# Range tests of the weights on their high halves and later in the order; the first chunk's scores of both halves in pairs

## The chip, the core and the metric

One core of a Trainium2 chip. The metric is the device time of one execution in microseconds; three runs of the kernel before gave 1187.11, 1194.1 and 1196.09, median 1194.1.

## The reference, cut to what matters

Three parts follow each other. First a recurrence over 768 steps for 4 x 8 heads, each with a 40 x 40 state:

```
for t in range(S):
    y[t]  = einsum('d,de->e', r[t], state)
    Sa    = einsum('de,e->d', state, a[t])
    state = state * w[t][None, :] - outer(Sa, b[t]) + outer(v[t], k[t])
```

Its output, laid out as 3072 tokens x 320, goes through two dense layers without normalisation. The first is `h = x @ w_in; g = h * cos(h); x = g @ w_out` with 2048 hidden values, the second `h = x @ w_in2; g = s * max(h, 0)**2 + b; out = g @ w_out2`.

## The kernel before, in words

The recurrence is computed in 12 chunks of 64 steps. A chunk is prepared (decay products by a scan on DVE, scaled inputs, scores between steps as matmuls, an inverse of a triangular system on DVE), and then goes through a chain that carries the state to the next chunk. The 32 heads stand as two halves of the partitions (rows 0 to 39 and 64 to 103) times two pair groups `pg` times eight; a "g" is one half of one pair group. `prep` lists the preparation, `chain` the chain. Behind the chain the 64 x 4 tokens of the chunk are stored (`xs`), reloaded (`x1_load`) and go through the first dense layer (`m1_f`: the product with `w_in`, cosine, split in high and low halves; `m1_s`: the product with `w_out`). The second dense layer (`x2`, `m2_f`, `m2_s`) runs when all chunks are through.

Matmuls run in float16 with operands split in a high and a low half, except for chunk 0, whose scores, transposes and chain use float32 operands of 40 rows directly. For chunk 0, `sc1` (k, b against a) and `sc2` (the transposed result XT against r) are run once for each g, eight matmuls of 40 x 128 weights and 64 columns, all on one half of the rows.

The weights arrive as 64-bit floats. `float32` rebuilds 32-bit words on DVE with three integer instructions, in place; `w_in_chunk` and `w_out_chunk` then take a range test, copy the high half (ACT), scale (POOL) and subtract to get the low half (POOL or DVE). The range test is a Square on ACT with a running sum into `st`; for `w1` the squares also feed short matmuls with a vector of ones (`norm`, PSUM tile `np`) and a maximum on DVE. The sums are looked at once, at the end (`verdict`), to choose between this program and a slow one. Raw chunks lie partly in the place of the final weights and partly in four buffers of the tag "xs", which also holds the reloaded tokens.

The order of the work is written out by a planner, `Recorder`, when the program is built: every operation gets an estimated duration, a priority (its longest path to the end) and the time at which its inputs are there; `schedule` picks, engine by engine, the operation that can start first, by priority where several can. The engines then run their lists strictly in that order, and SP issues all transfers in one order. `caps` limits how many tiles of a class live at once ("XT": 2), out of shared buffers such as the eight of tag "q". All recorded instructions carry line 392 of the program, so rows are told apart by tile names: `w`, `v`, `wraw`, `vraw` are weights, `junk` the sink of squares, `s1p` and `s2p` the scores of `sc1` and `sc2`, `txp` and `XT` the transposes before `sc2`, `hp` and `op` the two products of a dense layer, `q`, `gh`, `gl` the hidden values and their halves, `yhl` the halves of y, `x` the stored tokens.

Of the kernel before, what the change touches and what calls it, by code (L numbers as in the profile page):

```python
# [24 lines left out]
C = 64  # L25
# [63 lines left out]


class _Op:
    __slots__ = ("eng", "calls", "dur", "lat", "blk", "preds", "succ", "npred", "prio", "ready", "tiles", "start", "end", "idx", "mm", "cols")


class Recorder:
# [5 lines left out]
    def __init__(self, nc, caps):  # L101
        self.real, self.caps = nc, caps
        for e in self.ENG:
            setattr(self, e, _Engine(self, e))
        self.ops, self.blk = [], -1
        self.base = {}
        self.sink = set()
        self.blk_tiles = {}
        self.key = {}
        self.acc = {}  # L110
        self.use = {}
        self.free = {}
        self.n_bufs = {}
        self.live_cls = {}
        self.order = {}
        self.t_eng = dict.fromkeys(self.ENG, 0.0)
        self.done_blk = set()
        self.todo = []
        self.cols = {}
        self.t_dma = 0.0  # L120

    def pool(self, p, name):
        return _Pool(self, p, name)
# [26 lines left out]
    @staticmethod  # L150
    def cost(eng, method, out, ins, k):
        size = lambda x: math.prod(c for _, c in list(x.ap)[1:])
        n = size(out)
        psum = any(x.space == PSUM for x in ins)
        if eng == "tensor":

            k, m, f = ins[0].ap[0][1], size(ins[0]), 1 + (ins[0].dtype == F32)
            if method == "transpose":
                return k * f, m * f, k / 128, k * f * f
            low = Recorder.region(out)[0] < 64  # L160
            n, side = size(ins[1]) * f * f, 2 if m <= 64 else 1
            return n if low else 0, (32 if m == 128 and f == 1 else m * f * f) / side, k / 128, n / side
        if eng == "scalar":
            return (0.05 if psum else 0.092) + n * 0.833e-3 + (0.093 if k.get("accum_out") is not None else 0) + \
                (0.093 if isinstance(k.get("bias"), bass.AP) else 0)
        if eng == "vector":
            if method == "reciprocal":
                return 0.065 + n * 6.3e-3
            if method == "tensor_tensor_scan":
                return 0.065 + n * 2.08e-3  # L170
            if method == "transpose":
                return 0.065 + n * 1.87e-3
            if method == "tensor_reduce":
                return 0.065 + size(ins[0]) * 1.04e-3
            half = method in ("tensor_scalar", "tensor_copy", "memset") and not (psum and ins[0].dtype == F32)
            return 0.065 + n * (0.52e-3 if half else 1.04e-3) + (0.063 if isinstance(k.get("scalar"), bass.AP) else 0)
        if eng == "gpsimd":
            if method in ("tensor_scalar", "memset"):
                return 0.05 + n * (1.03e-3 if method == "tensor_scalar" else 0.8e-3)
            return 0.147 + n * (2.1e-3 if out.dtype == F32 else 1.887e-3)  # L180
        b = WIDTH.get(out.dtype, 4) * math.prod(c for _, c in out.ap)
        run = min(Recorder.run(x) for x in (out, *ins) if x.ap[-1][0] == 1)
        full = max(x.ap[0][1] for x in (out, *ins) if x.space != DRAM) == 128
        return 0.45 if full else 0.625, b / (360e3 if run >= 512 else 180e3)
# [11 lines left out]
    def add(self, eng, method, f, a, k):  # L196
# [7 lines left out]
        if not (op is not None and eng == "tensor" and op.eng == eng and op.blk == self.blk):  # L204
            op = _Op()
            op.eng, op.calls, op.dur, op.lat, op.blk = eng, [], 0.0, 0.0, self.blk
            op.preds, op.succ, op.tiles, op.ready, op.idx = {}, [], set(), 0.0, len(self.ops)
            op.start = op.end = None
            self.ops.append(op)
            self.todo.append(op)  # L210
            op.mm, op.cols = [], 0
        op.calls.append((f, a, k))
        if eng == "sync":
            op.dur, op.mm = c
# [60 lines left out]
    def schedule(self, until=None):  # L275
# [22 lines left out]
        while n_left and left:  # L298
            best = None
            for e in self.ENG:  # L300
                te = self.t_eng[e]
                pick = None
                for o in ready[e]:
                    est = max(o.ready, te)
                    if o.blk not in self.done_blk:
                        s = self.slots(o.blk)
                        if s is None:
# [124 lines left out]
class Fast:  # L432
# [5 lines left out]
    def consts(self, p):  # L438
# [14 lines left out]
        self.st = p.tile([128, len(STATS), 2 * NC], F32, name="st")  # L453
        nc.gpsimd.memset(self.st, 0.0)
        self.tmin = p.tile([128, 2, 16], F32, name="tmin")
        self.junk = p.tile([128, 512], BF16, name="junk")
        self.neg1 = p.tile([128, 1], F32, name="neg1")
        nc.gpsimd.memset(self.neg1, -1.0)
        self.half_pi = p.tile([128, 1], F32, name="half_pi")
# [100 lines left out]
    def w_in_chunk(self, dst, name, k, n, lo):  # L560
        nc = self.nc
        raw = self.RAW["i", k]
        st = self.float32(raw)
        if name == "w1":
            sq = raw.bitcast(BF16)[..., 0::4]
            nc.scalar.activation(sq, st, AF.Square, accum_out=self.st[0:120, STAT_IX[name], k:k + 1])
            self.norm(self.ones, [sq[0:j, i] for i, j in enumerate((120, 120, 80))], k, 1)
        else:
            for q in (0, 2):
                self.square(st[:, q:min(q + 2, 3)], name, 2 * k + q // 2)  # L570
        m = n // 128
        wv = dst[:, k * m:k * m + m].rearrange("p f a n -> p a f n")
        sv = st.rearrange("p a (f n) -> p a f n", f=m)
# [6 lines left out]
    def w_out_chunk(self, dst, name, k):  # L580
        nc = self.nc
        st = self.float32(self.RAW["o", k])
        self.square(st, name, k)
        nc.scalar.activation(dst[:, k, 0], st, AF.Copy, scale=SW)
        if name == "v2" and k % 4 < 2:
            nc.vector.scalar_tensor_tensor(out=dst[:, k, 1], in0=st, scalar=SW, in1=dst[:, k, 0], op0=ALU.mult, op1=ALU.subtract)
            return
        nc.gpsimd.tensor_scalar(out=st, in0=st, scalar1=SW, scalar2=1.0, op0=ALU.mult, op1=ALU.mult)
        nc.gpsimd.tensor_tensor(out=dst[:, k, 1], in0=st, in1=dst[:, k, 0], op=ALU.subtract)

    def weights(self, wn, vn, wd, vd):
        for k in range(0, NFF, 2):
# [21 lines left out]
    def scan(self, c):  # L614
        nc = self.nc
        for q in range(2):
            nc.scalar.activation(self.junk.rearrange("p (l j) -> p l j", j=32), self.X[c][0][:, q * 16:q * 16 + 16, 1:33], AF.Relu,
                                 bias=self.neg1, accum_out=self.st[:, STAT_IX["w"], 2 * c + q:2 * c + q + 1])
        for y, op in zip(self.X[c], (ALU.subtract, ALU.add)):
            y = y.rearrange("p l j -> p (l j)")  # L620
# [112 lines left out]
    def sc1(self, c, g):  # L733
        nc = self.nc
        ps = self.pp.tile([128, 8, C], F32, tag="at", bufs=8, name="s1p")
        for l in range(8):
            if c == 0:
                r = slice(g % 2 * 64, g % 2 * 64 + 40)
                k = self.IN["kb", c, g // 2][r, l].rearrange("p m t -> p (m t)")
                a = self.A0[g // 2, 0][r, l]  # L740
            else:
                k, a = self.KB[c, g][0:120, l, :], self.AR[c, g][0:120, l, 0:C]
            nc.tensor.matmul(ps[:, l, :], k, a, start=(l == 0), stop=True, skip_group_check=True)
        if g == 0:
            self.ND[c] = self.pst.tile([128, 16, 32], F32, tag="ND", name="ND", bufs=1)
        m = self.M1[c, g] = self.pa.tile([128, 8, C], F32, tag="M1", name="M1", bufs=7)
# [177 lines left out]
    def sc2(self, c, g):  # L924
        nc = self.nc
        ps = self.pp.tile([128, 8, C], F32, tag="at", bufs=8, name="s2p")
        for l in range(8):
            if c == 0:
                r = slice(g % 2 * 64, g % 2 * 64 + 40)
                x, ar = self.XT[0, g, l // 4][r, l % 4, :], self.A0[g // 2, 1][r, l, :]  # L930
            else:
                x, ar = self.XT[c, g][0:120, l, :], self.AR[c, g][0:120, l, C:2 * C]
            nc.tensor.matmul(ps[:, l, :], x, ar, start=(l == 0), stop=True, skip_group_check=True)
        m = self.M2[c, g] = self.pm.tile([128, 8, C], F32, tag="q", name="M2", bufs=8)
        nc.vector.tensor_tensor(out=m, in0=ps, in1=bc(self.mask2, 1, [128, 8, C]), op=ALU.mult)

# [180 lines left out]
    def prep(self, c):  # L1117
# [4 lines left out]
        for pg in range(2):  # L1122
# [3 lines left out]
            do(self.stage_ar, c, pg)  # L1126
            do(self.kb_out, c, 2 * pg)
            do(self.kb_out, c, 2 * pg + 1)
            for g in (2 * pg, 2 * pg + 1):
                do(self.tz, c, g)  # L1130
                do(self.sc1, c, g)
        do(self.inv_begin, c)
        do(self.inv, c)
        do(self.inv_out, c)
# [4 lines left out]

    def chain(self, c, pg):  # L1140
        g0, g1 = 2 * pg, 2 * pg + 1
        for f in [(self.rhs, c, pg), (self.u_half, c, pg, 0), (self.lmul, c, pg), (self.u_half, c, pg, 1), (self.uhl, c, g0), (self.uhl, c, g1),
                  (self.sp, c, pg), (self.tx, c, g0), (self.sc2, c, g0), (self.tx, c, g1), (self.sc2, c, g1),
                  (self.yt, c, pg), (self.ts, c, pg)]:
            self.do(*f)

# [11 lines left out]
    def run(self, es0):  # L1158
# [3 lines left out]
        with ExitStack() as es:  # L1162
# [2 lines left out]
            self.x0 = dr.tile([NC, 2, 3, 40, 768], F16, name="x0")  # L1165
            self.x1 = dr.tile([NC, 2, 128, DM], F32, name="x1")
            self.consts(pc)
            rec = self.nc = Recorder(nc, {"any": {"at", "xs", "q"}, "cls": {"XT": 2, "rhp": 3, "hp": 2, "op": 2, "xs": 2, "M2": 2, "q": 4, "att": 6}})
            rec.sink.add(self.junk.tensor.name)
            pool = lambda s, n, **k: rec.pool(s.enter_context(tc.tile_pool(name=n, bufs=1, **k)), n)  # L1170
            self.pm = pool(es, "mlp")
# [13 lines left out]
            for c in range(NC):  # L1185
# [6 lines left out]
                self.do(self.xs, c)  # L1192
                self.do(self.x1_load, c)
                self.mlp(self.m1_f, self.m1_s, c)
            rec.schedule(until=("prep",))
            es_p.close()
            es_v = ExitStack()
# [15 lines left out]
            for j in range(NC):  # L1213
                self.do(self.x2, j)
                self.mlp(self.m2_f, self.m2_s, j)
            rec.schedule()
            es_b.close()
            es_v.close()
# [158 lines left out]
```

## Time and profile before

| | us |
|---|---|
| runs | 1187.11, 1194.1, 1196.09 (median 1194.1) |
| profiled execution, its own time | 1188.45 |
| its span, first to last instruction | 1186.7 |
| busy: PE, weight loads, DVE, ACT, POOL | 1024.5, 822.7, 718.7, 740.1, 437.2 |
| chain that ended last: PE, DVE, DMA, ACT, SP's queue | 57%, 13%, 12%, 7%, 6% |

Busy times are sums over the whole span and don't say where an engine limits the work; the chain of waits gives shares by what was worked on last. Both are averages over stages, which the rows below take apart. A row's idle time is that of its engine just before it, with what ended it.

### The profile page before, as it was taken

How to read it: one execution, taken by the hardware profiler on the slowest of the kernel's cores; microseconds unless marked ns; L12 is line 12 of the kernel's file. 1: busy time of each engine (PE TensorE's matmuls, PEld its weight loads, DVE VectorE, ACT ScalarE, POOL GpSimd, SP SyncE). 2: the span in 40 equal slices, each digit the busy share in tenths (PEclk: the TensorE clock that was granted, in tenths of full speed). 3: DMA queues.
4: the chain of work that ended last, by engine and by line, in shares of the span. 5: the costliest groups of instructions: out<-in, count | busy, mean ns of one | idle time of the engine just before them, and what ended most of it. 6: DMA issues, size and time to landing. Idle time of an engine off the chain costs nothing.

```text
span 1186.7 us, 37912 instructions
## 1 busy us (share of the span) xinstructions
PE 1024.5 (86%) x16094; PEld 822.7 (69%) x16094; DVE 718.7 (61%) x1390; ACT 740.1 (62%) x1640; POOL 437.2 (37%) x430
## 2 busy tenths in 40 slices
PE   3335878988999889989989998976999999999996
PEld 3234767776778677767777776755788888888885
DVE  6989475857573849384846553789444455454543
ACT  4466568786767677677868674766544454444443
POOL 2685455465535464536454512358300000000000
PEclk9999969999999899989998899888999999999999
DMA  9553343444433543253443222475000000000001
GB/s 229 190 193 121 114 151 116 150 126 156 138 101 122 159 144 125 95 172 109 146 137 124 86 68 73 147 185 131 27 23 23 23 23 23 23 23 23 23 13 24
DMA packets 74755, 121.15 MB, mean 102 GB/s; under 512 B 16500, under 2 KB 47348, under 8 KB 73556
## 3 DMA queue, kind: packets, MB, share of 16 engines
q1 hardware_dynamic: 74580, 118.67, 33.1%
q8 instruction: 128, 2.10, 0.8%
q14 instruction: 47, 0.39, 0.1%
HBM read 72.71 MB, written 12.29 MB: 72 GB/s over the span
## 4 chain that ended last, share of the span: by engine, by line
PE 57%; DVE 13%; DMA 12%; ACT 7%; SPq 6%; issue 4%; POOL 0%; ACTq 0%; DVEq 0%; POOLq 0%
PE hp L392 23%; PE op L392 21%; SPq L392 6%; DMA XX<-in_w 4%; PE ytp L392 3%; PE rhp L392 3%; DVE XX L392 3%; DMA wraw<-in_w 3%; DVE wraw L392 2%; DMA XT<-XT 2%; PE uhp L392 2%; DVE v L392 1%; DMA xs<-x 1%; ACT XT L392 1%; DVE w L392 1%
## 5 line engine op out<-in xcount | busy, mean ns | idle before, releaser
L392 PEld LDWEIGHTS <-w 120*128 120x128 f16 (+1 forms) x3102 | 301.1, 100 | 98.8 <-ACT w L392 33.1
L392 PE MATMUL op<-v,gh 128*128 128x320 f16 x1536 | 328.5, 304 | 3.2 <-ACT gh L392 3.0
L392 PE MATMUL op<-v,gl 128*128 128x320 f16 x768 | 232.9, 303 | 2.6 <-POOL gl L392 2.6
L392 PE MATMUL hp<-xs,w 120*128 120x256 f16 x1536 | 208.8, 287 | 11.9 <-DMA xs<-x 10.7
L392 PE MATMUL hp<-x2s,w 120*128 120x256 f16 x1536 | 189.8, 272 | 0.0
L392 POOL TENSOR_TENSOR gl<-q,gh 128x512 f16<-128x512 f32 x96 | 116.9, 1220 | 197.0 <-ACT gh L392 191.8
L392 PEld LDWEIGHTS <-gh 128*128 128x128 f16 x1536 | 144.2, 99 | 52.2 <-ACT gh L392 3.6
L392 ACT ACTIVATE q<-hp 128x512 f32<-128x512 f32 x96 | 57.2, 596 | 126.3 <-PE hp L392 126.0
L392 DVE SCALAR_TENSOR_TENSOR q<-q,s_t 128x512 f32<-128x512 f32 x96 | 72.1, 751 | 102.6 <-ACT q L392 96.8
L392 DVE SCALAR_TENSOR_TENSOR q<-hp,q 128x512 f32<-128x512 f32 x96 | 65.3, 684 | 81.0 <-ACT q L392 78.3
L392 DVE SCALAR_TENSOR_TENSOR gl<-q,b_t,gh 128x512 f16<-128x512 f32 x96 | 72.1, 752 | 48.9 <-ACT gh L392 46.8
L392 PEld LDWEIGHTS <-gl 128*128 128x128 f16 x768 | 75.8, 99 | 35.2 <-POOL gl L392 3.8
L392 ACT ACTIVATE gh<-q,b_t 128x512 f16<-128x512 f32 x96 | 69.1, 720 | 42.9 <-DVE q L392 41.8
L392 DVE TENSOR_TENSOR_SCAN XX<-XX,starts 128x264 f32<-128x264 f32 x96 | 73.1, 816 | 29.2 <-DMA XX<-in_w 28.2
L392 ACT ACTIVATE q<-hp,half_pi 128x512 f32<-128x512 f32 x96 | 65.1, 681 | 36.4 <-PE hp L392 33.7
L392 POOL TENSOR_TENSOR kb<-kb,XX 128x512 f32<-128x512 f32 x44 | 57.6, 1318 | 73.2 <-DVE XX L392 64.1
L392 ACT ACTIVATE gh<-q 128x512 f16<-128x512 f32 x96 | 59.2, 625 | 22.2 <-DVE q L392 20.2
L392 POOL TENSOR_TENSOR kbl<-kb,kbh 128x1024 f16<-128x1024 f32 x22 | 47.5, 2158 | 28.0 <-ACT kbh L392 27.5
L392 ACT ACTIVATE R<-rhp 32x320 f32<-32x320 f32 x96 | 41.1, 428 | 23.1 <-PE rhp L392 21.0
L392 PE MATMUL rhp<-UF,M 64*64 64x40 f32 (+1 forms) x1536 | 53.3, 229 | 0.8 <-ACT UF L392 0.5
L392 DVE TENSOR_TENSOR M<-s2p,mask 128x512 f32<-128x512 f32 x48 | 32.2, 685 | 34.6 <-PE s2p L392 34.5
L392 POOL TENSOR_TENSOR arl<-ar,arh 128x1024 f16<-128x1024 f32 x22 | 48.0, 2180 | 12.3 <-ACT arh L392 12.2
(184 smaller groups left out, 1787.4 us busy)
## 6 DMA issues: line engine op xcount, KB each, us to landing
XX<-in_w SPq DMA_DIRECT2D x12, 1056.0 KB
kb<-in_kb SPq DMA_DIRECT2D x24, 512.0 KB
ar<-in_ar SPq DMA_DIRECT2D x22, 512.0 KB
KB<-kbh SPq DMA_DIRECT2D x88, 80.0 KB
ars<-arh SPq DMA_DIRECT2D x88, 80.0 KB
v<-in_v SPq DMA_DIRECT2D x20, 320.0 KB
wraw<-in_w SPq DMA_DIRECT2D x8, 720.0 KB
SS<-SHL SPq DMA_DIRECT2D x88, 50.0 KB
```

The source lines that it names most:

```text
L392: f(*a, **k)
```

## The change

The range tests leave the conversion of a chunk. New functions read the finished high halves, scaled back, two chunks at a time, and are recorded behind the first dense layer's work for chunk 3 (and, for the second layer, behind chunk 3 of its work), with a field `nb` that tells the planner not to start them before 250 us (750 us) plus 12 us a step, in its own time. For chunk 0, `sc1_0` and `sc2_0` put the matmuls of the two halves of a pair group in turn, into two PSUM tiles; what followed a score group stands in `sc1_end` and `sc2_end`. In the chain of chunk 0 both transposes come ahead of the scores. The class limit of XT is 3, the planner counts two row halves for matmuls of up to 64 rows, and the sink of squares has 640 columns.

```diff
-            n, side = size(ins[1]) * f * f, 2 if m <= 64 else 1
+            n, side = size(ins[1]) * f * f, 2 if m <= 64 or k <= 64 else 1
...
-                    est = max(o.ready, te)
+                    est = max(o.ready, te, o.nb)
...
     def w_in_chunk(self, dst, name, k, n, lo):
         st = self.float32(raw)
-        if name == "w1":
-            sq = raw.bitcast(BF16)[..., 0::4]
-            nc.scalar.activation(sq, st, AF.Square, accum_out=self.st[0:120, STAT_IX[name], k:k + 1])
-            self.norm(self.ones, [sq[0:j, i] for i, j in enumerate((120, 120, 80))], k, 1)
-        else:
-            for q in (0, 2):
-                self.square(st[:, q:min(q + 2, 3)], name, 2 * k + q // 2)
...
     def w_out_chunk(self, dst, name, k):
-        self.square(st, name, k)
...
+    def w_in_test(self, src, name, k):
+        sq = self.pm.tile([120, 2, 3, 128], BF16, tag="xs", name="wsq", bufs=4)
+        for i, (rows, a, n) in enumerate(((120, 0, 2), (80, 4, 1))):
+            nc.scalar.activation(sq[0:rows, :, 2 * i:2 * i + n], src[0:rows, 2 * k:2 * k + 2, a:a + n], AF.Square, scale=1.0 / SW,
+                                 accum_out=self.st[0:rows, STAT_IX[name], 2 * k + i:2 * k + i + 1])
+        if name == "w1":
+            for f in range(2):
+                self.norm(self.ones, [sq[0:j, f, i] for i, j in enumerate((120, 120, 80))], 2 * k + f, 1)
+    def w_out_test(self, src, name, k):
+        self.square(src[:, 2 * k:2 * k + 2, 0], name, k, 1.0 / SW)
+    def tests(self, wn, vn, wd, vd, t):
+        for k in range(NFF // 2):
+            self.nc.nb = t + 12 * k
+            self.do(self.w_in_test, wd, wn, k)
+            self.do(self.w_out_test, vd, vn, k)
+        self.nc.nb = 0.0
...
+    def sc2_0(self, pg):
+        ps = [self.pp.tile([128, 8, C], F32, tag="at", bufs=8, name="s2p") for _ in range(2)]
+        for l in range(8):
+            for hf in range(2):
+                r = slice(hf * 64, hf * 64 + 40)
+                self.nc.tensor.matmul(ps[hf][:, l, :], self.XT[0, 2 * pg + hf, l // 4][r, l % 4, :], self.A0[pg, 1][r, l, :],
+                                      start=(l == 0), stop=True, skip_group_check=True)
+        for hf in range(2):
+            self.sc2_end(0, 2 * pg + hf, ps[hf])
...
+        sc2 = [(self.tx, c, g0), (self.tx, c, g1), (self.sc2_0, pg)] if c == 0 else [(self.tx, c, g0), (self.sc2, c, g0), (self.tx, c, g1), (self.sc2, c, g1)]
...
-            rec = self.nc = Recorder(nc, {..., "cls": {"XT": 2, ...}})
+            rec = self.nc = Recorder(nc, {..., "cls": {"XT": 3, ...}})
...
                 self.mlp(self.m1_f, self.m1_s, c)
+                if c == 3:
+                    self.tests("w1", "v1", self.w1, self.v1, 250)
...
                 self.mlp(self.m2_f, self.m2_s, j)
+                if j == 3:
+                    self.tests("w2", "v2", self.w2, self.v2, 750)
```

`sc1_0` has the form of `sc2_0`, with the scaled k, b as weights and the scaled a as moving operand.

## Rows read from the trace of the kernel before

**Rows 1.** Busy time by stretch: start:end, length, each engine's busy us (instructions), granted clock, DMA.
```profile
0.00:90.00 90.00, 32.46 (x546) 28.77 (x546) 70.97 (x143) 47.29 (x125) 51.66 (x86) 1.00 0.71 206
90.00:175.00 85.00, 59.03 (x1010) 50.47 (x1009) 59.30 (x134) 54.68 (x138) 45.63 (x54) 0.90 0.41 128
175.00:760.00 585.00, 533.47 (x11125) 424.22 (x11123) 351.46 (x779) 419.95 (x919) 278.03 (x213) 0.95 0.40 126
250.00:346.00 96.00, 85.25 (x1677) 66.76 (x1675) 55.23 (x114) 68.52 (x152) 45.98 (x37) 0.95 0.43 136
```
**Rows 2.** Order of time, 150 to 176 us, all engines: start, length, engine, instruction.
```profile
153.40 0.69 DVE L392 SCALAR_TENSOR_TENSOR y<-ytp,XX 128x512 f32<-128x512 f32 x1 [2.31 <-PE ytp L392]
...
164.75 0.71 SPq L392 DMA_DIRECT2D x<-yhl  x2
...
169.76 0.44 SPq L392 DMA_DIRECT2D xs<-x  x1
...
174.64 1.67 PE L392 MATMUL hp<-xs,w 120*128 120x256 f16 x7
```
**Rows 3.** Order of time on PE, 75 to 160 us (float32 matmuls have two records each).
```profile
91.23 1.93 PE L392 MATMUL rhp<-UF,M 64*64 64x40 f32 x32
93.69 1.90 PE L392 MATMUL txp<-ident_f,UF 128*40 128x128 f32 x8 [0.52 <-ACT UF L392]
...
103.00 3.67 PE L392 MATMUL s2p<-ars,XT 40*128 40x64 f32 x16
...
127.56 1.89 PE L392 MATMUL txp<-ident_f,UF 128*40 128x128 f32 x8
...
135.12 3.67 PE L392 MATMUL s2p<-ars,XT 40*128 40x64 f32 x16
...
144.33 3.67 PE L392 MATMUL s2p<-ars,XT 40*128 40x64 f32 x16 [2.23 <-ACT XT L392]
```
**Rows 4.** Order of time on ACT, 70 to 200 us.
```profile
113.46 1.06 ACT L392 ACTIVATE wraw<-wraw 120x384 bf16<-120x384 f32 x1 [5.05 <-DVE wraw L392]
...
134.34 0.63 ACT L392 ACTIVATE XT<-txp 40x512 f32<-40x512 f32 x1
```
**Rows 5.** Waits of PE, 0 to 175 us: total us, times, longest.
```profile
PE np L392 <- ACT w L392: 32.4, 5, 17.9
...
PE np L392 <- ACT wraw L392: 9.2, 3, 6.0
```
**Rows 6.** Order of time on SP's queue, 70 to 170 us.
```profile
127.17 9.60 SPq L392 DMA_DIRECT2D w<-wlo  x3
136.94 0.86 SPq L392 DMA_DIRECT2D vraw<-in_v  x2
```
**Rows 7.** Groups of ACT by form, whole run: count, busy us, mean ns, idle before.
```profile
L392 ACT ACTIVATE w<-w 120x384 bf16<-120x384 f32 x10 | 10.3, 1070 | 19.3 <-DVE w L392 19.3
L392 ACT ACTIVATE junk<-v 128x320 bf16<-128x320 f32 x20 | 9.8, 488 | 10.1 <-DVE v L392 8.6 <-ACT v L392 1.0 <-ACT w L392 0.3
L392 ACT ACTIVATION_READ_ACCUMULATOR junk<-v 128x1 f32 x20 | 3.8, 189 | 0.0
L392 ACT ACTIVATION_READ_ACCUMULATOR w<-w 120x1 f32 x10 | 2.6, 261 | 0.0
L392 ACT ACT_TABLE_LOAD x2 | 2.6, 1283 | 8.8 <-DMA XX<-in_w 8.8
```
**Rows 8.** Chain that ended last, 690 to 870 us: start, us, what.
```profile
721.90 0.08 PE np L392 x4
```
**Rows 9.** Order of time on ACT, 190 to 197 us.
```profile
194.93 0.63 ACT L392 ACTIVATE ysq<-y 128x512 bf16<-128x512 f32 x1
195.45 0.20 ACT L392 ACTIVATION_READ_ACCUMULATOR ysq<-y 128x1 f32 x1
```
**Rows 10.** Waits of PE for ACT, 175 to 760 us, the two longest.
```profile
PE uhp L392 <- ACT o L392: 2.1, 1, 2.1
...
PE s1p L392 <- ACT q L392: 0.9, 1, 0.9
```
**Rows 11.** Groups by form, 690 to 860 us: DVE's conversion of the second layer's weights.
```profile
L392 DVE SCALAR_TENSOR_TENSOR wraw<-wraw 120x768 int32<-120x768 int32 x16 | 24.7, 1576 | 0.0
```

More of the change, by code (lines that the diff above doesn't have):

```diff
@@ L91 @@
 class _Op:
-    __slots__ = ("eng", "calls", "dur", "lat", "blk", "preds", "succ", "npred", "prio", "ready", "tiles", "start", "end", "idx", "mm", "cols")
+    __slots__ = ("eng", "calls", "dur", "lat", "blk", "preds", "succ", "npred", "prio", "ready", "tiles", "start", "end", "idx", "mm", "cols", "nb")
 class Recorder:
@@ L120, in __init__ @@
         self.t_dma = 0.0
+        self.nb = 0.0
     def pool(self, p, name):
@@ L210, in add @@
             self.todo.append(op)
-            op.mm, op.cols = [], 0
+            op.mm, op.cols, op.nb = [], 0, self.nb
         op.calls.append((f, a, k))
@@ L455, in consts @@
         self.tmin = p.tile([128, 2, 16], F32, name="tmin")
-        self.junk = p.tile([128, 512], BF16, name="junk")
+        self.junk = p.tile([128, 640], BF16, name="junk")
         self.neg1 = p.tile([128, 1], F32, name="neg1")
@@ L589, in w_out_chunk @@
         nc.gpsimd.tensor_tensor(out=dst[:, k, 1], in0=st, in1=dst[:, k, 0], op=ALU.subtract)
+    def w_in_test(self, src, name, k):
+        nc = self.nc
+        sq = self.pm.tile([120, 2, 3, 128], BF16, tag="xs", name="wsq", bufs=4)
[13 more added lines that the diff above has]
+        self.nc.nb = 0.0
     def weights(self, wn, vn, wd, vd):
@@ L616, in scan @@
         for q in range(2):
-            nc.scalar.activation(self.junk.rearrange("p (l j) -> p l j", j=32), self.X[c][0][:, q * 16:q * 16 + 16, 1:33], AF.Relu,
+            nc.scalar.activation(self.junk[:, 0:512].rearrange("p (l j) -> p l j", j=32), self.X[c][0][:, q * 16:q * 16 + 16, 1:33], AF.Relu,
                                  bias=self.neg1, accum_out=self.st[:, STAT_IX["w"], 2 * c + q:2 * c + q + 1])
@@ L736, in sc1, with sc1_0, sc1_end @@
         for l in range(8):
[L737 to L742, printed above, removed]
-            nc.tensor.matmul(ps[:, l, :], k, a, start=(l == 0), stop=True, skip_group_check=True)
+            k, a = self.KB[c, g][0:120, l, :], self.AR[c, g][0:120, l, 0:C]
+            nc.tensor.matmul(ps[:, l, :], k, a, start=(l == 0), stop=True, skip_group_check=True)
+        self.sc1_end(c, g, ps)
+    def sc1_0(self, pg):
+        ps = [self.pp.tile([128, 8, C], F32, tag="at", bufs=8, name="s1p") for _ in range(2)]
+        for l in range(8):
+            for hf in range(2):
+                r = slice(hf * 64, hf * 64 + 40)
+                k = self.IN["kb", 0, pg][r, l].rearrange("p m t -> p (m t)")
+                self.nc.tensor.matmul(ps[hf][:, l, :], k, self.A0[pg, 0][r, l], start=(l == 0), stop=True, skip_group_check=True)
+        for hf in range(2):
+            self.sc1_end(0, 2 * pg + hf, ps[hf])
+    def sc1_end(self, c, g, ps):
+        nc = self.nc
         if g == 0:
@@ L927, in sc2, with sc2_end @@
         for l in range(8):
[L928 to L933, printed above, removed]
+            nc.tensor.matmul(ps[:, l, :], self.XT[c, g][0:120, l, :], self.AR[c, g][0:120, l, C:2 * C], start=(l == 0), stop=True, skip_group_check=True)
+        self.sc2_end(c, g, ps)
+    def sc2_0(self, pg):
+        ps = [self.pp.tile([128, 8, C], F32, tag="at", bufs=8, name="s2p") for _ in range(2)]
+        for l in range(8):
+            for hf in range(2):
+                r = slice(hf * 64, hf * 64 + 40)
+                self.nc.tensor.matmul(ps[hf][:, l, :], self.XT[0, 2 * pg + hf, l // 4][r, l % 4, :], self.A0[pg, 1][r, l, :],
+                                      start=(l == 0), stop=True, skip_group_check=True)
+        for hf in range(2):
+            self.sc2_end(0, 2 * pg + hf, ps[hf])
+    def sc2_end(self, c, g, ps):
+        nc = self.nc
         m = self.M2[c, g] = self.pm.tile([128, 8, C], F32, tag="q", name="M2", bufs=8)
@@ L1128, in prep @@
             do(self.kb_out, c, 2 * pg + 1)
+            if c == 0:
+                do(self.sc1_0, pg)
             for g in (2 * pg, 2 * pg + 1):
                 do(self.tz, c, g)
-                do(self.sc1, c, g)
+                if c:
+                    do(self.sc1, c, g)
         do(self.inv_begin, c)
@@ L1141, in chain @@
         g0, g1 = 2 * pg, 2 * pg + 1
+        sc2 = [(self.tx, c, g0), (self.tx, c, g1), (self.sc2_0, pg)] if c == 0 else [(self.tx, c, g0), (self.sc2, c, g0), (self.tx, c, g1), (self.sc2, c, g1)]
         for f in [(self.rhs, c, pg), (self.u_half, c, pg, 0), (self.lmul, c, pg), (self.u_half, c, pg, 1), (self.uhl, c, g0), (self.uhl, c, g1),
-                  (self.sp, c, pg), (self.tx, c, g0), (self.sc2, c, g0), (self.tx, c, g1), (self.sc2, c, g1),
+                  (self.sp, c, pg), *sc2,
                   (self.yt, c, pg), (self.ts, c, pg)]:
@@ L1167, in run @@
             self.consts(pc)
-            rec = self.nc = Recorder(nc, {"any": {"at", "xs", "q"}, "cls": {"XT": 2, "rhp": 3, "hp": 2, "op": 2, "xs": 2, "M2": 2, "q": 4, "att": 6}})
+            rec = self.nc = Recorder(nc, {"any": {"at", "xs", "q"}, "cls": {"XT": 3, "rhp": 3, "hp": 2, "op": 2, "xs": 2, "M2": 2, "q": 4, "att": 6}})
             rec.sink.add(self.junk.tensor.name)
```

## Prediction

> **What bounds the kernel now.** I read first the table by stages, to see where TensorE (PE) idles; then each engine's order of work in the stretch with the most idle time; then the list of waits.
>
> The table [rows 1] shows three regimes. Up to 90 us PE is busy 32.5 of 90 us while VectorE (DVE) is busy 71: the weights are being converted and chunk 0 scanned. From 90 to 175 us PE is busy 59 of 85, so 26 us are idle. From 175 to 760 us it is busy 533.5 of 585, or 91%: there the kernel is bound by PE, and work or waiting added off PE mostly disappears. What ends the second regime is the first matmul of the first dense layer at 174.6 us [rows 2]. It is the last link of a chain: y of chunk 0's second half at 153.4, its store issued at 164.75, the reload at 169.8, the matmul behind that. So the question for this change is how much sooner chunk 0 gets through, and what is paid for that in the PE-bound stretch.
>
> How chunk 0 gets through stands in PE's order [rows 3]. Each half pair goes through a transpose (1.9 us for 8), ScalarE copies (XT), and a group of scores (3.67 us for 8 heads, 0.46 us a matmul), head group by head group: transpose, scores, transpose, scores. The second pair has its first transposes at 127.6, its scores at 135.1 and 144.3. Between them ScalarE (ACT) was in the way: the XT copy at 134.34 comes right after the range test of a weight chunk, and the test at 113.46 had itself stood 5.05 us for DVE's conversion, with everything behind it on ACT [rows 4]. The same tests feed PE's norm matmuls (np), and PE waits for those in order, 32.4 us in 5 places and 9.2 us in 3 [rows 5]; most of the first sum falls where PE has little else to do (17.9 us in one place).
>
> **The change, part by part.** *Tests of the first layer's weights leave the start.* Removed from ACT: 16 squares of 1.07 us with 0.26 us to read the sum, and 16 of 0.49 with 0.19 [rows 7]: 16 x 1.33 + 16 x 0.68 = 32 us, with 48 norm matmuls on PE and 16 short reductions on DVE, all before 167 us. ACT is busy 102 of the first 175 us [rows 1], so the 32 us are not worth 32; they are worth what waited behind them. That is the copies to high halves, then GpSimd (POOL), then SP's queue: at 127.2 SP needs 9.6 us for three transfers of low halves, and the next two raw chunks leave only at 136.9 [rows 6]. Up to four squares, 5.3 us, lie in that stretch. So the weights come some 4 to 6 us sooner; I count this only as what lets the next part count.
>
> *Chunk 0 in pairs.* From rows 3: with both transposes (3.8 us) ahead of the scores, the second pair's XT is complete at about 127.6 + 3.8 + 1.2 = 132.6 (the copies run beside the transposes, the last two behind them; 0.6 us each is my estimate). The paired scores then take 3.7 us if two 40-row matmuls on different halves of the rows run beside each other, or 7.3 if not. I take the first. The nearest row that alternates between halves is 64x64: 16 such matmuls (32 records) take 1.93 us, 0.12 us each [rows 3], at about a quarter of the 0.46 us of a score with 128 columns, where half the columns alone would give a half. The scores end at 136.3 (or 139.9) where they ended at 148.0; y follows 5.4 us behind as it does now, at 141.7 (or 145.3) instead of 153.4: 8.1 to 11.7 us. For the first pair the same sum gives scores done at 98.8 + 3.7 = 102.5 (or 106.1) against a second group that starts only behind the tests; how much of that the second pair can use depends on the order that the planner writes. Bounds for the first dense matmul: 4 us sooner (one group of scores, 3.67, and nothing else) to 30 (11.7, and some 18 from the first pair). I take 16, nearest to the sum for the second pair with a third of the first. The scores of k and a (32 matmuls of the same form) lie before 35 us, under DVE's 71 busy us [rows 1]: nothing, and if DVE weren't there, 7 us.
>
> Of 16 us I let 15 reach the end: 91% busy behind it, and a start that comes sooner fills idle PE time, of which there are 26 us between 90 and 175 [rows 1].
>
> *The same tests in the PE-bound stretch.* They come back from the planner's 250 us on, every 12 us, eight groups. PE: 48 norm matmuls at 0.08 us for four in a dense stretch [rows 8]: +1. ACT: per group a square of 512 (0.63 with 0.20 for the sum [rows 9]), one of 256 (at most 0.49 + 0.19), one of 640 (between 0.63 and 0.98, plus 0.19): about 2.4 us, 19 us in all. ACT is busy 68.5 of the 96 us there [rows 1], and 87 with them. Queued behind each group are the copies of hidden values (gh), which release POOL and then PE. PE waits for ACT seldom in the whole stretch from 175 to 760 (the longest is 2.1 us [rows 10]). Bounds 0 to 19; I take +2, near the low end because the waits are so few.
>
> *The second layer's tests.* 16 squares of v (10.8 us by rows 7) and those of w leave the conversion stage, and come back from 750 us on, later in the stage and partly in the last stretch, where ACT has room. The stage is set by DVE's conversions (24.7 us in 16 instructions alone [rows 11]), so I take -1, between -10.8 and +2.
>
> *The third XT buffer and a new order.* The limit rises for all chunks, and the whole order is planned again. No row prices that; I take 0, and 5 us either way, a tenth of the 51.5 us that PE idles from 175 to 760 [rows 1].
>
> Sum: -15 + 1 + 2 - 1 = -13 us. The profiled execution took 1188.45, which gives 1175.5; it lies 5.65 under the median of the three runs, 1194.1, and against that the forecast is **1181**.
>
> A rule that speaks against the move: squares now run among the Sin calls of the first dense layer. In the trace a square (ysq) already stands between a Sin and the next copy with nothing loaded [rows 9], and there are two table loads of 1.283 us in the whole run [rows 7]. The Trainium skill, page "ScalarE: Activation LUTs", section "What ACT_TABLE_LOAD costs", says that every switch to a different table set costs about 2.66 us with its drain; by that rule eight groups switched out and back would cost 16 x 2.66 = 43 us, an estimate from that page, and the time 1224. The trace speaks against a switch here.
>
> **The rivals.** *Slower: the tests land in PE's way.* Place: ACT between 250 and 346. Each group of 2.4 us is issued in one block; hidden values behind it are late, POOL after them, and PE drains. Price: up to 19 us, and 1 for the norms, with the start giving only its low bound of 4: 1194.1 + 16 - 1 = 1209. It decides from the point where over 16 of the 19 us reach PE. For it: ACT is at 71% there and would be at 90%. Against: rows 10, and a backlog of two pairs of hidden blocks between the layers' matmuls.
>
> *The start is not shortened.* DVE's conversions and the raw transfers hold the first dense matmul as they do now: chunk 0 is sooner, but the store waits in SP's order (it was issued 11 us behind y [rows 2]). Then +1 +2 -1 and 0 to -4: about 1194.
>
> *Much sooner.* Both pairs get through as soon as rows 3 allow, and the first dense matmuls run while the last weights come: 27 of 30 us arrive, 1167.
>
> *The pairs don't overlap.* Then two groups of 3.67 are back in the sum: 1181 + 7 = 1188.
>
> *A table switch*, priced by the loads of rows 7: 16 x 1.283 = 20.5 us, 1202.
>
> **How the numbers follow.** This kernel's measurement tells about 1%, 12 us, from no change: faster is below 1182, slower above 1206. Forecast 0.56, with its own range 1171 to 1190 (a start gain of 8 to 25 and the 5 us of the order): 0.36 of it faster, 0.20 same. Much sooner 0.10, faster. Not shortened 0.11 and no overlap 0.06, same. Tests in the way 0.16: 0.15 slower, 0.01 same. Table switch 0.01, same. Together faster 0.46, same 0.39, slower 0.15. The range is 1165 to 1200: below it lies a part of the much sooner case (0.04), above it most of the slower one (0.13).
>
> **What would show it.** Right: the first dense matmul at 150 to 166 us; no square of weights on ACT and no norm wait on PE for w before it; the 16 score matmuls of two groups in about 3.7 us rather than 7.3; eight groups of tests behind 250 us with PE's busy share there still near 89%; two table loads. Wrong: the first dense matmul still at 170 or later; the busy share between 250 and 350 us falling by several points with waits for ACT; score pairs at 7 us; more idle time of PE between 175 and 760 than the 51.5 us of before, which would mean that the new order gave the gain back.

## The result and the profile after

The changed kernel takes 1176.15 us in the median (four runs, 1173.57 to 1177.86); the kernel before took 1195.09 in the same comparison. The ratio is 0.985, 95% interval 0.981 to 0.989: 18.9 us, 1.6% of the median, faster, and clear of the noise. The forecast was 1181 and a gain of 13, with a range of 1165 to 1200.

The two profiled executions differ by less: 1188.45 and 1177.86, since that of before is one of its quicker ones (6.6 below its median) and that of after is not (1.7 above). Traces can show 10.6 us here; the other 8 lie between executions.

The stretches of the changed kernel, in the form of [rows 1]:

```profile
0.00:90.00 90.00, 27.90 (x577) 24.29 (x578) 68.45 (x136) 38.87 (x98) 49.05 (x86) 1.00 0.72 198
90.00:175.00 85.00, 55.24 (x1032) 45.26 (x1031) 64.41 (x145) 48.24 (x112) 42.32 (x46) 0.61 0.45 140
175.00:760.00 585.00, 538.54 (x11196) 427.25 (x11195) 364.13 (x818) 438.79 (x980) 289.92 (x233) 0.95 0.40 129
250.00:346.00 96.00, 89.18 (x1690) 69.36 (x1688) 62.65 (x147) 71.54 (x163) 45.18 (x34) 0.91 0.44 141
```

PE is busy less before 175 us (83.1 against 91.5), ACT too (87.1 against 102.0), and PE a little more from 175 to 760, where it idles 46.5 us for 51.5 before. The last conversions on DVE and the chain behind them, answering to [rows 2] (order of time, 136 to 162 us):

```profile
138.26 2.18 DVE L393 SCALAR_TENSOR_TENSOR wraw<-wraw 120x384 int32<-120x384 int32 x4
140.37 0.68 DVE L393 SCALAR_TENSOR_TENSOR y<-ytp,XX 128x512 f32<-128x512 f32 x1
...
146.24 0.86 SPq L393 DMA_DIRECT2D x<-yhl  x2
...
154.25 0.45 SPq L393 DMA_DIRECT2D xs<-x  x1
160.41 1.89 PE L393 MATMUL hp<-xs,w 120*128 120x256 f16 x8
```

Chunk 0's second pair on PE, answering to [rows 3]: both transposes stand ahead, and both groups of scores run as one.

```profile
123.90 3.60 PE L393 MATMUL txp<-ident_f,UF 128*40 128x128 f32 x16
...
128.92 2.00 PE L393 MATMUL s2p<-ars,XT 40*128 40x64 f32 x32
...
134.13 1.93 PE L393 MATMUL ytp<-M,Z 128*40 128x64 f32 x30 [0.16 <-DVE M L393]
```

The granted clock is 0.50 (1.2 GHz) from 119.9 to 128.9 us, in which PE is busy 8.99 of 9.02 us, and 1.00 (2.4 GHz) over the scores. In the kernel before the clock column reads 1.00 over [rows 3], yet a group of scores takes 3.67 us with weight loads of 330 ns, as in a run at a granted 0.50 (pairs only, below). The column first leaves 1.00 at about 158 us in that trace; ahead of that the durations tell the level, not the column.

Of PE's waits before 175 us that for the weights' norms [rows 5] is gone, but not its time: one wait for ND (chunk 0's inverse on DVE) is now 36.3 us, for 4.7 before. For XT PE waits 6.7 us, 5.7 of them in the first pair:

```profile
PE ydp L393 <- DVE ND L393: 36.3, 1, 36.3
...
PE s2p L393 <- ACT XT L393: 6.7, 2, 5.7
```

Chunk 0's y is there 13.0 us sooner (140.4 for 153.4), and the first dense matmul starts at 160.4 for 174.6: 14.2 us sooner. The tests in their new place (groups of ACT by form, whole run):

```profile
L393 ACT ACTIVATE junk<-v 128x640 bf16<-128x640 f16 x16 | 11.6, 725 | 0.1
L393 ACT ACTIVATE wsq<-w 120x512 bf16<-120x512 f16 x16 | 9.9, 619 | 0.0
L393 ACT ACTIVATE wsq<-w 80x256 bf16<-80x256 f16 x16 | 6.5, 403 | 0.0
...
L393 ACT ACT_TABLE_LOAD x2 | 2.6, 1283 | 8.8 <-DMA XX<-in_w 8.8
```

With 0.19 us to read each sum a group takes 2.3 us (forecast 2.4). Still two table loads. The first layer's groups land at 332 to 431 us on the chip, not at the planner's 250 to 334: the chip is some 90 us behind the planner's time there. From 339 to 435 us PE is busy 86.9 of 96 us (87.3 before), and its waits there are small:

```profile
PE np L393 <- ACT wsq L393: 2.7, 4, 0.9
PE hp L393 <- DMA xs<-x: 2.1, 1, 2.1
```

One wait is new. At the turn between the layers PE stands 18 us for the reload of the last chunk's tokens (SP's queue, then PE):

```profile
774.82 0.70 SPq L393 DMA_DIRECT2D x<-yhl  x2
778.53 3.61 SPq L393 DMA_DIRECT2D wraw<-in_w  x4
782.18 0.60 SPq L393 DMA_DIRECT2D xs<-x  x1
```
```profile
777.78 0.30 PE L393 MATMUL op<-v,gl 128*128 128x320 f16 x1
796.12 1.25 PE L393 MATMUL hp<-xs,w 120*128 120x256 f16 x5 [18.03 <-DMA xs<-x]
```

While the store (x) lands, SP issues four raw loads of 720 KB each; the 360 KB reload goes out behind them at 782.2 and is there at 796. Before, the same order of issues cost 2.7 us, as PE still had the chunk ahead to finish.

### The profile page after: what moved, and what is told of

Its sections match the earlier page's. It is cut to its first block, busy times and chain, and to the rows that moved or that the text cites. A ratio compares the mean times of both kernels' runs of the same rounds, so it can differ in the third digit from the quotient of the medians.

```text
span 1176.1 us, 37866 instructions
## 1 busy us (share of the span) xinstructions
PE 1005.3 (85%) x16094; PEld 805.7 (69%) x16094; DVE 705.5 (60%) x1390; ACT 729.6 (62%) x1608; POOL 430.1 (37%) x430
## 4 chain that ended last, share of the span: by engine, by line
PE 56%; DMA 10%; DVE 8%; ACT 6%; SPq 3%; issue 3%; POOL 2%; ACTq 0%; DVEq 0%; POOLq 0%
PE hp L393 22%; PE op L393 21%; SPq L393 3%; PE rhp L393 3%; DMA XX<-in_w 2%; PE ytp L393 2%; PE uhp L393 2%; DMA x2f<-x 2%; DVE XX L393 1%; DVE wraw L393 1%; PE spp L393 1%; PE txp L393 1%; DMA vraw<-in_v 1%; DMA ars<-arl 1%; ACT XT L393 1%
## 5 line engine op out<-in xcount | busy, mean ns | idle before, releaser
L393 PEld LDWEIGHTS <-w 120*128 120x128 f16 x3072 | 297.6, 100 | 75.3 <-DMA xs<-x 24.0
L393 PE MATMUL hp<-xs,w 120*128 120x256 f16 x1536 | 206.0, 285 | 23.9 <-DMA xs<-x 22.6
L393 DVE TENSOR_TENSOR_SCAN XX<-XX,starts 128x264 f32<-128x264 f32 x96 | 69.3, 774 | 22.8 <-DMA XX<-in_w 21.5
L393 PEld LDWEIGHTS rhp<-UF,M 64*64 64x64 f32 (+1 forms) x1536 | 48.5, 140 | 16.5 <-ACT UF L393 11.0
L393 DVE TENSOR_TENSOR M<-s1p,mask 128x512 f32<-128x512 f32 x48 | 32.3, 682 | 39.3 <-PE s1p L393 39.2
```

Of the source, the lines that this page charges most:

```text
L393: f(*a, **k)
```

## Experiments

All against the kernel before, in medians. "First dense" is the start of the first dense matmul, "middle" the time from there to the second layer's first matmul, "idle at the turn" what PE idles from the last store of y to that matmul; these three come from one profiled execution each, which is not always a typical one: that of pairs only took 10.4 us less than its median, that of the XT limit 8.5 more. From the second layer's first matmul to the end it is 346 to 355 us in all.

| kernel | median us | ratio (95%) | first dense | middle | idle at the turn |
|---|---|---|---|---|---|
| before | 1195 | | 174.6 | 665 | 14.5 |
| changed | 1176 | 0.985 (0.981 to 0.989) | 160.4 | 669 | 23.7 |
| tests only | 1205 | 1.009 (1.006 to 1.013) | 170.7 | 681 | 28.1 |
| pairs only | 1183 | 0.989 (0.985 to 0.993) | 166.7 | 656 | 19.3 |
| XT limit only | 1189 | 0.994 (0.991 to 0.997) | 165.1 | 682 | 24.9 |
| changed, halves apart | 1180 | 0.988 (0.983 to 0.993) | 159.2 | 673 | 25.0 |
| changed, no tests | 1184 | 0.990 (0.986 to 0.993) | 160.1 | 675 | 25.6 |
| changed, tests sooner | 1195 | 1.001 (0.998 to 1.004) | 157.4 | 689 | 24.4 |
| before, no tests | 1195 | 1.001 (0.998 to 1.004) | 170.6 | 673 | 24.9 |
| changed, held | 1170 | 0.982 (0.978 to 0.985) | 159.8 | 654 | 11.1 |
| pairs only, held | 1181 | 0.990 (0.986 to 0.994) | 170.0 | 661 | 17.8 |
| tests only, held | 1203 | 1.006 (1.003 to 1.009) | 171.8 | 675 | 18.9 |
| before, held | 1192 | 0.997 (0.995 to 1.000) | 176.3 | 660 | 16.7 |

How much of a difference is chance can be read from rows that share one order of work. Each kernel without the hold and the same one with it run the same instructions in the same order up to the turn, and so does halves apart beside the changed kernel; no tests and tests sooner share the changed kernel's order through the whole start. Within such a group the first dense matmul differs by 1 to 3 us, and the time from there to the last store of y by 3 to 7.

**Tests only.** The changed kernel with `sc1`, `sc2`, `prep`, `chain`, the XT limit and the planner's cost as before.

> The tests are moved as in the changed kernel; chunk 0's scores and transposes, the XT limit of 2 and the planner's cost stay as before. Theory A (the tests in the start's queues are what the change removes): about 1181, 14 us below before, first dense matmul at 162 to 166. Theory B (chunk 0's pairs are what shortens the start): about 1191, 4 us below before, first dense matmul at 170 or later. Theory C (the gain is the luck of a new order): no relation, anywhere from 1180 to 1205.

Slower by 11 us, outside theories A and B and at the end of C's range. First dense matmul 4 us sooner, y of chunk 0 at 153.37: not sooner at all, since the groups still stand in turn and PE waits for XT, as this order of time on PE shows:

```profile
131.19 1.89 PE L393 MATMUL txp<-ident_f,UF 128*40 128x128 f32 x8
...
143.47 3.69 PE L393 MATMUL s2p<-ars,XT 40*128 40x64 f32 x16 [9.09 <-ACT XT L393]
```

Theory A, mine in part, falls: freeing ACT of the tests does not by itself bring chunk 0 through. Theory B has the start right and the time wrong by 14 us. PE comes to the turn without a backlog and waits 19.6 us for the reload.

**Pairs only.** The changed kernel with `w_in_chunk` and `w_out_chunk` as before and no `tests`.

> Chunk 0's scores in pairs, both transposes ahead, the XT limit of 3; the tests stay in the conversion of each chunk. Theory A: about 1191, first dense matmul at 170 or later, with the norm waits of PE still there. Theory B: about 1180, first dense matmul at 160 to 164. Theory C: anywhere from 1180 to 1205.

12 us faster with the first dense matmul at 166.7 (170.0 in the same order with the hold): most of the gain, though less of the start than theory B said. The pair's price on PE is to be read here, at a granted clock of 0.50 and with the weight loads of 330 ns that [rows 3] have:

```profile
104.12 3.68 PE L393 MATMUL s2p<-ars,XT 40*128 40x64 f32 x32
```

Two groups in the time that one took (3.67).

**XT limit only.**

```diff
-"cls": {"XT": 2,
+"cls": {"XT": 3,
```

> The kernel before with the XT limit at 3 and nothing else. Theories A and B: within 5 us of before, 1190 to 1200, first dense matmul at 170 to 178. Theory C: a shift of 8 us or more either way, since only the order is new.

0.6% faster, 6 us, a little more than theories A and B allowed, and the first dense matmul is at 165.1, against them: 9.5 us sooner by the limit alone. The planner then puts both transposes ahead by itself:

```profile
132.03 3.60 PE L392 MATMUL txp<-ident_f,UF 128*40 128x128 f32 x16
136.68 4.10 PE L392 MATMUL s2p<-ars,XT 40*128 40x64 f32 x32 [1.05 <-ACT XT L392]
...
144.85 0.69 DVE L392 SCALAR_TENSOR_TENSOR y<-ytp,XX 128x512 f32<-128x512 f32 x1 [0.89 <-PE ytp L392]
```

y of chunk 0 is written at 144.85, 8.6 us sooner than before. With the halves one after the other, the 4.10 us for 32 records are those of the upper clock level for the most part (granted clock 0.80, median weight load 189 ns, where [rows 3] have 330). Pairs only holds this limit too, and its first dense matmul comes no sooner (166.7 and 170.0): with the tests in place, the pairing adds nothing to the start that the limit does not give.

**Halves apart.** In `sc1_0` and `sc2_0` the loop over halves stands outside:

```diff
-        for l in range(8):
-            for hf in range(2):
+        for hf in range(2):
+            for l in range(8):
```

> The changed kernel, with the eight score matmuls of one half of the rows ahead of the eight of the other, in place of one from each in turn; both transposes still ahead. If the turns are what lets two matmuls run beside each other: 7.3 us for 16 score matmuls at TensorE's lower clock level, y of chunk 0's second half 2 to 4 us later than 140.4, first dense matmul at 162 to 166, in all 1178 to 1184. If the hardware overlaps them in either order: 3.7 us, and 1173 to 1179.

PE does pay: the pair of groups at 127.3 takes 3.66 us where the changed kernel's at 128.9 takes 2.00, both mostly or wholly at the upper level (granted clock 0.90 and 1.00, median weight load 188 ns in each). But y is at 139.0 and the first dense matmul at 159.2, no later than with the turns (140.4, 160.4), and the medians' intervals overlap. In the order of time on PE and, at the end, on DVE, halves apart:

```profile
122.54 3.60 PE L393 MATMUL txp<-ident_f,UF 128*40 128x128 f32 x16
...
127.27 3.66 PE L393 MATMUL s2p<-ars,XT 40*128 40x64 f32 x32
...
136.91 2.18 DVE L393 SCALAR_TENSOR_TENSOR wraw<-wraw 120x384 int32<-120x384 int32 x4
139.02 0.68 DVE L393 SCALAR_TENSOR_TENSOR y<-ytp,XX 128x512 f32<-128x512 f32 x1
```

The reason stands on DVE. PE is done with y's matmuls (ytp) at 136.1 in the changed kernel and at 135.2 here, but y follows about 4 us later in both, straight behind DVE's conversions of raw weights, where before it waited for PE [rows 2]. So the turns save PE time (1.7 us here) that the path doesn't need. What shortens the start, beside the tests' leaving, is that both transposes, and all four XT copies, come ahead of the scores.

**No tests.** The changed kernel, squares, norms and maxima of the weights left out. The first try left the final decision without its sums, so that the slow program ran (19,053 us), and answers nothing; in the second the limits are opened (`"w1": (-1.0, 3.9)` and the same for the others).

> The changed kernel with the range tests of all four weights left out (their squares, norm matmuls and maxima): what the tests cost where they stand now. My prediction's terms of +2 and +1 for the first layer's and nothing for the second's: 3 us below the changed kernel, about 1173. The rival that they lie in PE's way: 10 us or more below it, 1166 or less, with PE's idle time between the first dense matmul and 760 us down by as much.

> The changed kernel with the range tests of all four weights left out, and their four limits opened so that the missing sums choose nothing. What the tests cost where they stand now. By my terms (+1 for PE, +2 for ACT, nothing for the second layer) about 1173, 3 us below the changed kernel; by the rival that they lie in PE's way 1166 or less.

1184, above both expectations, with an interval that overlaps that of the changed kernel from above: taking 27 us off ACT (729.6 to 702.4 us busy) and 48 matmuls off PE gains nothing that can be measured. The order is the changed kernel's up to 334 us, and another from there.

**Before, no tests.** The same left out of the kernel before.

> The kernel before with the range tests of all four weights left out and their limits opened. It has the start that the tests-only kernel has (first dense matmul at 170.7) and nothing in the dense stretch. If the 11 us that the moved tests cost on their own are paid where they now stand: 1189 to 1193, below before. If they come from the order and the turn between the layers, which a shorter start brings with it: 1198 or more, without a single test in the kernel.

No change, 1.001. A start that is 4 us shorter and 702 us of ACT for 740 give nothing at the end; PE waits 19.7 us for the reload at the turn. The result lies between the two cases: of the 11 us that the tests-only kernel loses, about 10 are not there without tests (intervals apart), and there is no gain either. The two kernels share their order up to about 315 us, where the tests set in.

**Tests sooner.** `self.tests("w1", "v1", self.w1, self.v1, 150)` in place of 250; the groups land at 198 to 316 us.

> The changed kernel with the first layer's tests allowed from the planner's 150 us on instead of 250, the second layer's as they were. The same instructions in another place. If the place decides (ACT in the dense stretch): the groups land some 100 us sooner, among the first chunks' work, and it takes 1182 or more. If the place is nearly free: 1172 to 1181, and what differs is the spread that a new order brings.

1195: the whole gain is gone. The start is no worse (157.4; its order is that of the changed kernel up to 203 us, so that the 3 us are chance), and the turn costs the same (PE waits 18.0 us for the reload in both). What grows is the stretch between, from the first dense matmul to the last store of y, here the changed kernel and then this one:

```profile
160.40:774.82 614.42, 564.55 (x11508) 447.75 (x11505) 383.57 (x864) 456.02 (x1011) 305.44 (x246) 0.94 0.39 125
157.40:792.95 635.55, 575.52 (x11508) 453.55 (x11505) 387.32 (x863) 456.58 (x1011) 306.46 (x246) 0.92 0.38 121
```

Of the 21 us, 11 are the same number of matmuls being busy longer, at a lower granted clock (0.92 for 0.94), and 10 are idle time of PE. No single wait there is longer than 3.6 us: the ones for state, XT, scores' inputs and UF each add a little.

**Held raw loads.** In the planner, the loads of the second layer's w may not be picked until the last `x1_load` is:

```diff
+                    if self.hold.get(o.blk, o.blk) not in self.done_blk and o.blk in self.hold:
+                        continue
...
                 self.do(self.w_in_load, self.i["w2"], self.w2, k)
+                rec.hold[rec.blk] = last
```

> The changed kernel, with the raw loads of the second layer's w held in the planner's order until the reload of the last chunk's tokens is issued. In the changed kernel that reload is issued behind four raw loads of 720 KB and PE stands 18 us for it. If the turn between the layers is where the changed kernel gives gain back: about 1166, 10 us below it, the wait for xs down to 5 us or less. If the raw loads themselves limit the turn (they start 4 us later here): no faster than the changed kernel, 1175 to 1180.

> The tests moved without chunk 0's pairs (which took 1205), with the same hold on the raw loads. If the 11 us that the moved tests cost on their own lie at the turn between the layers (19.6 us of waiting for xs): about 1190. If they lie among the first layer's work, behind the tests on ACT: 1200 or more still.

> The kernel before with the same hold. Its wait for xs at the turn was 2.7 us, since PE still had the products of the chunk ahead to do; so little is to be had: 1189 to 1196. If it gains 8 us or more, the turn costs every order the same and says nothing about the change.

> Chunk 0's pairs with the tests where they were, and the raw loads held behind the last reload of tokens. The pairs alone took 1183 with 7.2 us of waiting for that reload, so 1176 to 1180 if the hold only takes that wait away. If the moved tests bring anything beside the pairs, this stays above the changed kernel with the hold (1170) by 5 us or more; if they bring nothing, it comes to 1168 to 1173.

On the changed kernel the wait is gone: the reload goes out at 776.2, ahead of the raw loads, and PE waits 0.3 us for it.

```profile
771.01 0.70 SPq L396 DMA_DIRECT2D x<-yhl  x2
...
776.20 0.43 SPq L396 DMA_DIRECT2D xs<-x  x1
776.68 6.60 SPq L396 DMA_DIRECT2D wraw<-in_w  x6
```

Idle at the turn falls from 23.7 to 11.1 us and the turn itself from 54.8 to 42.9, but the second layer takes 353 us for 346.5, because conversions now run into it (DVE is busy 176 us there for 164, POOL 18.8 for 5.4, and PE waits 4.2 us for POOL's gl). The median is 1170: faster than the kernel before by 1.8%. Its interval overlaps the changed kernel's, so that it beats that one is not shown. On the kernel before the hold gives 0.3%, at the edge of what can be told, as expected. The tests-only kernel stays at 1203: the turn is not the main part of its loss, and that expectation fell. Pairs with the hold come to 1181, 11 us above the changed kernel with it: there the moved tests do bring something, intervals apart (0.986 to 0.994 against 0.978 to 0.985).

## Why the prediction was right, step by step

*Chunk 0 sooner: right in size, half right in cause.* The first dense matmul came 14.2 us sooner, where 16 were taken and 4 to 30 bounded. The sum for the second pair gave y at 141.7; it came at 140.4, and that this is so near is luck. The transposes began 3.7 us sooner than in the sum (123.9 for 127.6) and the scores were done at 130.9 instead of 136.3, helped by the upper clock level; then y followed 9.5 us behind them, not 5.4, because DVE's conversions stood in front of it. And I set the gain on the overlap of two row halves ("I take the first", 3.7 us rather than 7.3). The overlap is real (3.68 us for two groups) and not what counts (halves apart: 159.2). The step that carries it is the one that I passed over with a rise of a limit that "no row prices": XT at 3 lets the second transposes go ahead, and that alone gave 9.5 us in its one profiled execution. What the planner's new cost for two row halves does by itself was not run.

*Tests leaving the start: right in size.* 4 to 6 us forecast for the weights, counted only as what lets the rest count. Alone they gave 4 us at the first dense matmul, and at the end nothing (left out) or a loss of 11 us (moved); with the pairs the first dense matmul moves on from 166.7 to 160.4.

*15 of 16 us reach the end: true here, not in general.* Of 14.2 us, 10.6 reach the end in the traces; by the medians the gain of 18.9 is more than the start gave. Between the first dense matmul and the second layer's first one the changed kernel needs 669 us and the kernel before 665, with PE busy 596 us in both: up to the last store of y PE idles 5 us less, at the turn 9 more. Other orders needed 654 to 689 for nearly the same work: before without tests loses its 4 us of start, tests sooner all of its 17.

*A new order: badly undersized.* I took 5 us either way, a tenth of the idle time. The middles of the table spread over 35 us; part of it is the turn, where the idle time ranges from 11 to 28. Up to the last store alone the orders take 599 us (pairs only) to 636 (tests sooner), where executions of one order differ by 3 to 7. This is the term of the sum that was mis-sized, and that it came out at only 4 us for this change is luck.

*Tests in the dense stretch: +3 is not contradicted.* Norms wait 2.7 us in all for squares; leaving all tests out gains nothing. The rival that they lie in PE's way is not what happened in the changed kernel. Without the pairs it is not refuted: there the moved tests cost 10 us against the same start without tests (1205 and 1195), they or the order that came with them. With the groups at 198 to 316 us the kernel is 19 us slower; whether ACT in that place does it or the order that came with it is open, since no run has that order without the tests.

*The second layer's tests: -1 for a turn that got 5 us shorter.* It went from 60.0 to 54.8 us, with ACT busy 22 us in it for 39; but PE idles 9 us more, behind the reload. So part of the gain turned into a new wait there, worth 12.6 us of idle time by the held kernel; in its median it is 6 us, which the intervals don't separate from nothing.

*The table rule.* Two loads of 1.283 us, as before: no switch. By the Trainium skill's page "ScalarE: Activation LUTs", section "What ACT_TABLE_LOAD costs", a switch to another set would have shown a load of 1.283 us each. The trace agrees in the length of a load and has none between Squares and Sins, so Square is served beside Sin in this program.

What stays open: the 8 us by which the medians differ more than the profiled executions, why moved tests cost 11 us on their own and help with the pairs held, and the spread of the middle, which no single wait explains and in which the granted clock has a part.

## What to carry to other kernels

Ask which limit on live buffers writes the order, before asking what a faster matmul is worth: a limit of two tiles had put transposes behind scores, and lifting it alone shortened the start by 9.5 us, while nearly halving the scores' time on PE moved nothing, as y stood behind other work on DVE by then. A list planner's new order is itself a term of the sum; where every edit replans everything, its spread is measured (here some 35 us in one stretch, against 3 to 7 between executions of one order), not guessed as a tenth of the idle time. And a small reload that a stage waits for is worth trying ahead of the next stage's bulk loads in the queue, above all once the work that used to cover it is done sooner: here that took away a wait of 18 us, though a gain in the median is not shown.

## What the runs showed of the hardware

Two float32 matmuls of 40 rows and 128 columns on different row halves, one in turn with the other, take the time of one (3.68 us for 16 against 3.67 for 8, with weight loads of 330 ns in both), and run one half after the other they take 1.8 times as long (3.66 us at a granted clock of 0.90 against 2.00 at 1.00). The reload of 360 KB took 14 us from issue to arrival behind four transfers of 720 KB, at 235 GB/s over that stretch; issued ahead of the raw loads it took 5 us.
